# A decode step of attention and a dense layer: the result on four partitions of two column groups, two stores, and held weights for w2's last row

## The chip, the core and the metric

The kernel runs on one core of a Trainium2 chip. Such a core has a matrix engine (TensorE, in the profile PE, its weight loads PEld), a vector engine (VectorE, DVE), a scalar engine (ScalarE, ACT), GpSimd (POOL), and SyncE (SP), which here issues nearly all transfers. The engines run side by side, each through its own queue in order, and wait for each other on semaphores. SBUF is the working memory of 128 partitions; PSUM, also of 128 partitions, takes what TensorE computes. The metric is the time of one execution on the device in microseconds (us). A profiled execution has a time of its own, and a span, which is the part of it that the trace shows.

## The reference

Two batch rows, one new token each. `A` is attention over a cache of 4096 positions with 32 heads of 128, `B` a dense layer with ReLU, and a gate mixes the two.

```python
def _A_ref(x, k_cache, v_cache, wq, wo):        # x 2x1x512, caches 2x32x4096x128
    q = (x @ wq).reshape(B, Sq, Hq, Dh) -> b h q d
    scores = jnp.einsum("bhqd,bhkd->bhqk", q, k) * (Dh ** -0.5)
    p = _softmax(scores, axis=-1)
    o = jnp.einsum("bhqk,bhkd->bhqd", p, v)
    return o.transpose(0, 2, 1, 3).reshape(B, Sq, Hq * Dh) @ wo
def _B_ref(x, w1, w2):                          # w1 512x1376, w2 1376x512
    return jnp.maximum(x @ w1, 0) @ w2
g = _sigmoid((A_x * gate_w).sum(-1, keepdims=True))
return g * a + (1 - g) * b                      # 2x1x512, bf16
```

## The kernel before

Every operation is recorded by a helper in the queue of its engine, in the order in which the code is written; a named marker becomes a semaphore value that others wait for. There is no planner: the written order is the order of each queue.

SP issues the loads one after the other (L282 to L295): wq, w1, twenty-one pieces of the K and V caches, the first 96 rows of w2 (`w2x`, two transfers of twelve rows in SBUF from a three by four cut in DRAM, L289), wo in two parts (rows 0 to 23 and 24 to 31 of each partition's 32, `WO_CUT` = 24), and the rest of w2 in three parts (`w2b` rows 0 to 6, `w2c` rows 7 and 8, `w2d` row 9). Pieces share regions of one SBUF buffer, so each load waits until the piece before it in its region has been read; w2's last parts wait only for their turn. The store is SP's last transfer (L296), and SP then waits for it to be received (L298).

The computation: `gate` makes the gate and some constants on VectorE from an identity matrix that POOL fills in (L232 to L260, a list of memsets and selects; `sel2`, a two-column selector, is reduced on VectorE in L326). `q_proj` and `ffn_h` are the first products; `ffn_relu` (L406) writes the hidden row of the dense layer, already multiplied with 1 - g, into `hT` (128 partitions, 14 columns, 2 batch rows). Then 64 turns of K: VectorE transposes (L417), TensorE makes scores. Softmax, then eleven pieces of V: products on TensorE (L510), extraction on VectorE (L518, L521).

The tail, in TensorE's order, after V's last piece:

- `project(range(-4, 0))`: the four rows of `w2x` with `hT`, into one PSUM bank, each row in one column group of the array (`tile_position=(0, 32 * t)`, result on partitions 32t and 32t+1), 512 columns wide (L564).
- `o_gather`, `o_scale`, `o_turn`: the attention result, normed and gated, is turned and cast by VectorE (L552) into `oW` (128 partitions, 32 rows, 2 batch rows).
- `project(range(24))`: wo's rows 0 to 23 in the same way into the same bank (L564), which VectorE then copies to SBUF as `pr_sb` in fp32 (`pr_copy`, L569).
- `last_rows`: `fin_row` for wo's rows 24 to 31, then one for `pr_sb` with `sel2` (it adds the four column groups of the bank; fp32), then ten for w2's rows 0 to 9 with `hT`. Each `fin_row` is four matmuls of 128 columns (L573): the c-th quarter of the 512 outputs goes through column group c onto partitions 32c and 32c+1. Every matmul brings its own weight load, two columns.
- `store`: four casts of 2x128 from PSUM to `out_sb` (2x512), two after each other on VectorE (L592) and two on ScalarE (L594). Each raises the semaphore `fin`; SP stores at 4.

`mm_held` (L421) makes a matmul that uses the weights already in the array; the products with `xTw` and the K scores use it. A weight load of its own is `ldweights`.

Of the kernel before, what the change touches and what calls it, by code (L numbers as in the profile page):

```python
# [14 lines left out]
HALF = 16384  # L15
REGION = {"A": 0, "Ah": HALF, "B": 2 * HALF, "C": 4 * HALF}
WO_CUT = 24


class _Marker:  # L20
# [67 lines left out]
def bass_gated_mix__gqa_block_cached__dense_activation_relu__decode_kernel(  # L88
# [50 lines left out]
    nrow = sb("nrow", [128, 8, 4], dt.float32)  # L139
    negm = sb("negm", [128, 32], dt.float32)  # L140
    lsum = sb("lsum", [128, 2, 2], dt.float32)
    sel2 = sb("sel2", [128, 2], dt.float32)
    lrow = sb("lrow", [128, 2], dt.float32)
    rinv = sb("rinv", [32, 2], dt.float32)
    mask8 = sb("mask8", [128, 8], dt.bfloat16)
# [3 lines left out]
    sell_odd = sell[:, 1:65].rearrange("p (u f two) -> p u f two", u=8, two=2)[:, :, :, 0]  # L149
    s4 = sb("s4", [32, 4, 128], dt.bfloat16)  # L150
    O_sb = sb("O_sb", [32, 2, 128], dt.bfloat16)
    oW = sb("oW", [128, 32, 2], dt.bfloat16)
    hT = sb("hT", [128, 14, 2], dt.bfloat16)
    out_sb = sb("out_sb", [2, 512], dt.bfloat16)
    w2x = sb("w2x", [128, 4, 512], dt.bfloat16)
    hrowT = kt[:, 2, 0:448]

# [21 lines left out]

    for e in ("pe", "dve", "act", "pool"):  # L180
        P.sems[e] = nc.alloc_semaphore(e + "_ev")
    names = ["x", "gw", "wq", "w1", "wo0", "wo1", "w2x", "w2b", "w2c", "w2d", "out", "fin"]
    sem = {n: nc.alloc_semaphore("sem_" + n) for n in names}
    sem_region = {r: nc.alloc_semaphore("sem_region" + r) for r in REGION}

# [7 lines left out]
        return m  # L193


    both, lo, hi = (0, 1), (0,), (1,)
    k_pieces = [(0, both, "A"), (1, both, "B"), (2, lo, "C"), (3, both, "A"), (4, both, "B"), (2, hi, "C"),
                (5, both, "A"), (6, both, "B"), (7, lo, "C"), (7, hi, "A")]
# [30 lines left out]
    def pe(fn, waits=(), signal=None, dwaits=()):  # L229
# [4 lines left out]
    pool(lambda g: g.affine_select(out=ident16[:], in_=ident16[:], pattern=[[-1, 128]],  # L234
                                   compare_op=ALU.not_equal, fill=1.0, base=0, channel_multiplier=1),
         waits=["c_i16z"], signal="c_i16")
    pool(lambda g: g.memset(xTw[:], 0.0), signal="c_xTw")
    pool(lambda g: g.memset(qbuf[:], 0.0), signal="c_qbuf")  # L238
    pool(lambda g: g.memset(mpad[:], 0.0), signal="c_mpad")
    pool(lambda g: g.memset(w2x[:], 0.0), signal="c_w2x")  # L240
    pool(lambda g: g.memset(sell[:], 0.0), signal="c_s0")  # L241
    pool(lambda g: g.memset(sell_odd, 1.0), waits=["c_s0"], signal="c_s1")
# [50 lines left out]
    sp(lambda e: e.dma_start(wreg[:, 512 * WO_CUT:HALF], wo_in[:, 512 * WO_CUT:HALF]).then_inc(sem["wo1"], 16))  # L293
    for name, r0, r1 in (("w2b", 0, 7), ("w2c", 7, 9), ("w2d", 9, 10)):
        sp(lambda e, name=name, r0=r0, r1=r1: e.dma_start(w2[:, r0:r1, :], w2_in[:, r0:r1, :]).then_inc(sem[name], 16))  # L295
    sp(lambda e: e.dma_start(out.rearrange("b s n -> (b s) n"), out_sb[:, :]).then_inc(sem["out"], 16),  # L296
       dwaits=[(sem["fin"], 4)])
    sp(lambda e: e.wait_ge(sem["out"], 16))  # L298


    def gate():
        for t in range(4):
            pe(lambda e, t=t: e.transpose(PSB[0:128, XT_B0 + 4 * t:XT_B0 + 4 * t + 3], x_sb[0:3, t::4], ident16[0:3, 0:3]),  # L303
               waits=(["c_i16"] if t == 0 else []), dwaits=([(sem["x"], 16), (sem["gw"], 16)] if t == 0 else []),
               signal=("pe_xT" if t == 3 else None))
        dve(lambda v: v.tensor_copy(out=xT3[:, :, 0:3], in_=PSB[0:128, XT_B0:XT_B0 + 16].rearrange("p (t b) -> p t b", t=4)[:, :, 0:3]),  # L306
            waits=["pe_xT"], signal="dve_xT")
        dve(lambda v: v.tensor_copy(out=xTw[:, :, 0:2], in_=xT), waits=["dve_xT", "c_xTw"], signal="dve_xTw")
        dve(lambda v: v.tensor_tensor(out=xg[:], in0=xT, in1=xT3[:, :, 2:3].to_broadcast([128, 4, 2]), op=ALU.mult),
            waits=["dve_xT"], signal="dve_xg")  # L310
        dve(lambda v: v.tensor_reduce(out=xgs[:], in_=xg[:].rearrange("p t b -> p b t"), axis=AX.X, op=ALU.add),
            waits=["dve_xg"], signal="dve_xgs")
        pe(lambda e: e.matmul(psf(0, 128, G_C0, 2), lhsT=ones32[:, :], rhs=xgs[:, :], start=True, stop=True),
           waits=["dve_xgs", "c_ones"], signal="pe_z")
        act(lambda a: a.activation(out=ez[:], in_=psf(0, 128, G_C0, 2), func=ACT.Exp, scale=-1.0),
            waits=["pe_z"], signal="act_ez")
        dve(lambda v: v.tensor_scalar(out=ez1[:], in0=ez[:], scalar1=1.0, scalar2=None, op0=ALU.add),
            waits=["act_ez"], signal="dve_ez1")
        dve(lambda v: v.reciprocal(out=gb[:], in_=ez1[:]), waits=["dve_ez1"], signal="dve_g")
        dve(lambda v: v.tensor_scalar(out=gm[:], in0=gb[:], scalar1=-1.0, scalar2=1.0, op0=ALU.mult, op1=ALU.add),  # L320
            waits=["dve_g"], signal="dve_gm")
        dve(lambda v: v.tensor_reduce(out=maskc[:], in_=ident16[:].rearrange("p (k c) -> p c k", c=4), axis=AX.X, op=ALU.add),
            waits=["c_i16"], signal="dve_maskc")
        dve(lambda v: v.tensor_reduce(out=selx[:, 24:32], in_=ident16[:].rearrange("p (t h c) -> p h t c", t=4, c=4),
                                      axis=AX.XY, op=ALU.add), waits=["c_i16", "c_selx"], signal="dve_selx")
        dve(lambda v: v.tensor_reduce(out=sel2[:], in_=ident16[:].rearrange("p (t q) -> p q t", t=4)[:, 0:2, :], axis=AX.X, op=ALU.add),  # L326
            waits=["c_i16"], signal="dve_sel2")

    def q_window(b, blk, par, u):
        h = 2 * (blk % 2) + par  # L330
# [72 lines left out]
    def ffn_relu():  # L403
        dve(lambda v: v.transpose(out=hrowT, in_=psf(0, 128, HR_C0, 448)), waits=["pe_h"], signal="dve_hrT")
        for b in range(2):
            dve(lambda v, b=b: v.tensor_scalar(out=hT[:, :, b], in0=hrowT[:, b:448:32], scalar1=0.0,  # L406
                                               scalar2=gm[:, b:b + 1], op0=ALU.max, op1=ALU.mult),
                waits=["dve_hrT", "dve_gm"], signal=f"dve_h{b + 1}")


    def k_turn(i):
# [6 lines left out]
            waits=([f"pe_sc_{i - NKT}"] if i >= NKT else ["dve_h2"] if i == 2 else []), dwaits=([landed["k", n]] if first else []),  # L418
            signal=(f"k_read_{n}" if turn_end[n] == i else f"kt_{i}"))

    def mm_held(e, out, lhsT, rhs, start, stop, size=(128, 128), at=(0, 0)):  # L421
        a = e.lower_ap(rhs)
        w = e.lower_ap(lhsT, for_matmul_weights=True)
        return e.add_instruction(mybir.InstMatmult(  # L424
            start_tensor_calc=start, stop_tensor_calc=stop, tile_size=size, tile_position=at, ldweights=False,
            name=nc.get_next_instruction_name(), engine=mybir.EngineType.PE, ins=[a, w], outs=[e.lower_ap(out)]))

    def k_scores(i):
# [118 lines left out]
    def o_turn():  # L547
        for dq in range(4):
            pe(lambda e, dq=dq: e.matmul(psf(0, 128, R_C0, 64), lhsT=s4[:, dq, :], rhs=O_sb[:, :, 32 * dq:32 * dq + 32],
                                         start=(dq == 0), stop=(dq == 3), tile_position=(0, 0)),  # L550
               waits=(["dve_O0", "dve_O1", "c_s4"] if dq == 0 else []), signal=("pe_R" if dq == 3 else None))
        dve(lambda v: v.tensor_copy(out=oW[:, :, :].rearrange("p r b -> p b r"), in_=psf(0, 128, R_C0, 64).rearrange("p (b r) -> p b r", b=2)),  # L552
            waits=["pe_R"], signal="dve_oW")

    def pr_clear():
        dve(lambda v: v.memset(psf(0, 128, PR_C0, 512), 0.0), waits=["act_exp3"], signal="dve_pr0")
# [1 line left out]
    def project(rows):  # L558
        for r in rows:
            t = r % 4  # L560
            lhsT, rhs = (hT[:, 14 + r, :], w2x[:, t, :]) if r < 0 else (oW[:, r, :], wreg[:, r * 512:(r + 1) * 512])
            dw = {-4: [(sem["w2x"], 32)], 0: [(sem["wo0"], 16)]}.get(r, [])
            waits = {-4: ["dve_h2", "dve_pr0"], 0: ["dve_oW"]}.get(r, [])
            pe(lambda e, t=t, r=r, lhsT=lhsT, rhs=rhs: e.matmul(psf(32 * t, 32 * t + 2, PR_C0, 512), lhsT=lhsT, rhs=rhs,  # L564
                                                               start=(r < 0), stop=(r >= WO_CUT - 4), tile_position=(0, 32 * t)),
               dwaits=dw, waits=waits, signal=("pe_pr" if r == WO_CUT - 1 else None))

# [1 line left out]
        dve(lambda v: v.tensor_copy(out=pr_sb, in_=psf(0, 128, PR_C0, 512)), waits=["pe_pr"], signal="dve_pr")  # L569

    def fin_row(first, last, lhsT, rhs, dw, waits, signal):
        for c in range(4):
            pe(lambda e, c=c: e.matmul(psf(32 * c, 32 * c + 2, FIN_C0, 128), lhsT=lhsT, rhs=rhs[:, c * 128:(c + 1) * 128],  # L573
                                       start=first, stop=last, tile_position=(0, 32 * c), skip_group_check=True),
               dwaits=(dw if c == 0 else []), waits=(waits if c == 0 else []), signal=(signal if c == 3 else None))

    def last_rows():
        for r in range(WO_CUT, 32):
# [1 line left out]
        fin_row(False, False, sel2[:, :], pr_sb, [], ["dve_pr", "dve_sel2"], None)  # L580
        for r in range(10):
            dw = {0: [(sem["w2b"], 16)], 7: [(sem["w2c"], 16)], 9: [(sem["w2d"], 16)]}.get(r, [])
            fin_row(False, r == 9, hT[:, r, :], w2[:, r, :], dw, [], "pe_fin" if r == 9 else None)

    def store():
        def piece(c):
            return out_sb[:, 128 * c:128 * c + 128], psf(32 * c, 32 * c + 2, FIN_C0, 128)

        for c in range(4):
            dst, src = piece(c)  # L590
            if c < 2:
                dve(lambda v, dst=dst, src=src: v.tensor_copy(out=dst, in_=src).then_inc(sem["fin"], 1), waits=["pe_fin"])  # L592
            else:
                act(lambda a, dst=dst, src=src: a.activation(out=dst, in_=src, func=ACT.Copy).then_inc(sem["fin"], 1), waits=["pe_fin"])  # L594


    gate()
# [64 lines left out]
```

## Time and profile before

| what | us |
|---|---|
| time, median of 3 runs | 344.44 (344.37 to 344.48) |
| profiled execution: its time | 344.36 |
| profiled execution: its span in the trace | 343.0 |
| TensorE busy | 199.7 |
| VectorE busy | 192.9 |
| ScalarE busy | 15.0 |
| POOL busy | 9.5 |
| transfers: 145.43 MB read, over the span | 424 GB/s |
| mean granted clock of TensorE, share of full speed | 0.806 |

The table gives busy times of engines that work side by side, so they don't add up to the span. The 1.4 us between span and time lie before the first and after the last recorded instruction. The page lists the chain of work that ended last: followed back from the last instruction, each step goes to what released it. The share of a line in that chain, not its busy time, tells what it contributes to the time. A timeline line has the start from the span's begin, the duration, engine, line, operation, result and operands with their shapes (128x512 is partitions by elements), a count, and in brackets the idle time before it with what ended it. SPq and ACTq are the issuing of transfers by SP and ACT. The end of a matmul is modelled, its start is recorded.

### The profile page before, as it was taken

What the parts mean: (1) busy time and instruction counts of PE and PEld (TensorE: products, weight loads), DVE (VectorE), ACT (ScalarE), POOL (GpSimd) and SP (SyncE); (2) the same over time, 40 slices, a digit from 0 to 9 for tenths busy, and PEclk for the clock granted to TensorE, in tenths of its full rate; (3) what the DMA queues carried; (4) which work ended last, traced back from release to release, by engine and by line L of the source; (5) the groups of instructions that cost most, each with busy time, mean ns of one, the idle gap of its engine ahead of it and who ended that gap; (6) DMA issues with size and microseconds to landing.
All of it is one profiled execution on the core that took longest, in us unless ns stands there. A gap on an engine that the chain in (4) does not pass through costs nothing.

```text
span 343.0 us, 2484 instructions
## 1 busy us (share of the span) xinstructions
PE 199.7 (58%) x1232; PEld 52.2 (15%) x952; DVE 192.9 (56%) x136; ACT 15.0 (4%) x54; POOL 9.5 (3%) x21
## 2 busy tenths in 40 slices
PE   0440596998797996988999274005065043143656
PEld 0110121111111111111111031002023011021312
DVE  0240896996998996989999596304016103031221
ACT  1040001010001001000000300000000000000000
POOL 8200000000000000000000000000000000000000
PEclk9995599899898999999999767558568656587656
DMA  7998989999999989999999999999999999999996
GB/s 306 470 489 367 489 367 426 432 482 413 443 428 426 485 383 466 390 417 430 428 428 478 436 407 482 405 459 407 405 428 461 420 443 436 397 434 436 419 418 243
DMA packets 4081, 145.57 MB, mean 424 GB/s; under 512 B 459, under 2 KB 592, under 8 KB 872
## 3 DMA queue, kind: packets, MB, share of 16 engines
q1 hardware_dynamic: 4066, 145.43, 98.5%
q8 instruction: 8, 0.13, 0.2%
q14 instruction: 1, 0.01, 0.0%
q10 hardware_dynamic: 6, 0.00, 0.0%
HBM read 145.43 MB, written 0.00 MB: 424 GB/s over the span
## 4 chain that ended last, share of the span: by engine, by line
DMA 65%; PE 17%; DVE 15%; ACT 1%; SPq 0%; issue 0%; DVEq 0%
DMA kv<-in_A_k_cache_dram 27%; DMA kv<-in_A_v_cache_dram 26%; DVE kt L417 12%; DMA kv<-in_B_w_dram 8%; PE PS L510 5%; PE PS L424 5%; PE PS L445 5%; DMA kv<-in_A_wq_dram 4%; PE PS L344 1%; DVE kt L492 1%; ACT kt L465 1%; DVE qrow L368 1%; DVE mpad L453 1%; DVE kt L469 0%; PE PS L371 0%
## 5 line engine op out<-in xcount | busy, mean ns | idle before, releaser
L417 DVE STREAM_TRANSPOSE kt<-kv 128x2048 f32<-128x2048 f32 x64 | 141.1, 2273 | 23.0 <-DMA kv<-in_A_k_cache_dram 23.0
L445 PE MATMUL PS<-kt,qbuf 128*128 128x512 bf16 x256 | 106.1, 414 | 32.8 <-DVE kt L417 27.8
L424 PE MATMUL PS<-kt,qbuf 128*128 128x512 bf16 x256 | 105.5, 412 | 0.0
L510 PE MATMUL PS<-kv,kt 128*32 128x512 bf16 x512 | 46.1, 534 | 90.0 <-DMA kv<-in_A_v_cache_dram 77.1
L518 DVE TENSOR_TENSOR qbuf<-PS,maskc 128x512 f32<-128x512 f32 x11 | 7.6, 692 | 95.8 <-PE PS L510 95.7
L445 PEld LDWEIGHTS PS<-kt,qbuf 128*128 128x128 bf16 x256 | 25.6, 100 | 141.7 <-DVE kt L417 72.8
L510 PEld LDWEIGHTS PS<-kv,kt 128*32 128x32 bf16 x512 | 17.7, 125 | 116.8 <-issue 74.8
L492 DVE TENSOR_TENSOR kt<-kt,mask 128x512 bf16<-128x512 bf16 (+1 forms) x17 | 19.3, 1179 | 0.0
L339 ACT ACTIVATE qbuf<-PS 32x4 bf16<-32x4 bf16 (+1 forms) x40 | 7.6, 190 | 107.9 <-PE PS L424 105.9
L521 DVE TENSOR_REDUCE qbuf<-qbuf 128x128 f32<-128x512 f32 x11 | 11.3, 1025 | 0.4
L344 PE MATMUL PS<-kv,xTw 128*32 128x512 bf16 (+1 forms) x32 | 5.3, 690 | 3.3 <-DMA kv<-in_A_wq_dram 3.3
L594 ACT ACTIVATE out_sb<-PS 2x128 bf16<-2x128 f32 x2 | 0.5, 271 | 144.6 <-PE PS L573 144.6
L537 PE MATMUL PS<-qbuf,selx 128*32 128x128 f32 x22 | 4.9, 387 | 2.0 <-DVE qbuf L521 2.0
L368 DVE CAST qrow<-PS 128x256 bf16<-128x256 f32 x2 | 2.6, 1516 | 5.5 <-PE PS L424 5.5
L465 ACT ACTIVATE kt<-PS,negm 128x512 bf16<-128x512 f32 x4 | 2.7, 686 | 58.9 <-DVE negm L461 58.9
L303 PE MATMUL PS<-ident,x_sb 3*128 3x3 bf16 x4 | 0.3, 166 | 8.1 <-POOL sell L241 8.1
L306 DVE COPY xT<-PS 128x12 bf16<-128x12 bf16 x1 | 0.2, 170 | 8.4 <-PE PS L303 8.4
L238 POOL MEMSET qbuf<- 128x5120 bf16 x1 | 4.4, 4361 | 0.0
L537 PEld LDWEIGHTS PS<-qbuf,selx 128*32 128x32 f32 x22 | 3.4, 162 | 4.6 <-DVE qbuf L521 3.2
L424 PE MATMUL PS<-kv,xTw 128*32 128x512 bf16 (+1 forms) x24 | 3.7, 511 | 0.0
L453 DVE TENSOR_REDUCE mpad<-PS 128x2 f32<-128x2048 f32 x1 | 2.3, 2291 | 2.2 <-PE PS L424 2.2
L469 DVE STREAM_TRANSPOSE kt<-kt 128x1024 bf16<-128x1024 bf16 x2 | 2.5, 1246 | 1.6 <-ACT kt L465 1.5
(67 smaller groups left out, 32.3 us busy)
## 6 DMA issues: line engine op xcount, KB each, us to landing
kv<-in_A_v_cache_dram SPq DMA_DIRECT2D x6, 4096.0 KB, 36.9
kv<-in_A_k_cache_dram SPq DMA_DIRECT2D x4, 4096.0 KB, 31.7
kv<-in_A_wq_dram SPq DMA_DIRECT2D x1, 4096.0 KB, 12.2
kv<-in_A_wo_dram SPq DMA_DIRECT2D x1, 3072.0 KB, 23.4
kv<-in_B_w_dram SPq DMA_DIRECT2D x1, 1376.0 KB, 15.1
kv<-in_A_wo_dram SPq DMA_DIRECT2D x1, 1024.0 KB, 25.5
kv<-in_B_w_dram SPq DMA_DIRECT2D x1, 896.0 KB, 27.2
kv<-in_B_w_dram SPq DMA_DIRECT2D x1, 256.0 KB, 27.4
```

What stands on the lines that cost most here:

```text
L339: act(lambda a: a.activation(out=out, in_=src, func=ACT.Copy), waits=waits, signal=f"q_{b}_{u}_{blk}_{par}")
L344: return e.matmul(out, lhsT=xTw[:, t, :], rhs=rhs, start=(t == 0), stop=(t == 3), tile_position=(0, 32 * c))
L368: dve(lambda v, dst=dst, src=src: v.tensor_copy(out=dst, in_=src), waits=[f"pe_qr{half}"], signal=f"qrow{half}{e2}")
L417: dve(lambda v: v.transpose(out=dst, in_=pairs[:, h, 64 * a:64 * a + 64, :]), waits=([f"pe_sc_{i - NKT}"] if i >= NKT else ["dve_h2"] if i ...
L424: return e.add_instruction(mybir.InstMatmult(start_tensor_calc=start, stop_tensor_calc=stop, tile_size=size, tile_position=at, ldweights=F ...
L445: return e.matmul(out, lhsT=lhsT, rhs=rhs, start=start, stop=stop)
L465: act(lambda a, g=g, par=par: a.activation(out=E_sb[:, 32 * g:32 * g + 32, 16 * par:16 * par + 16], in_=psf(0, 128, (2 * par + g) * BANK, ...
L492: dve(lambda v: v.tensor_tensor(out=out, in0=src.unsqueeze(2).to_broadcast(shape), in1=mask8[:].unsqueeze(1).unsqueeze(3).to_broadcast(sha ...
L510: pe(lambda e, j=j, t=t: e.matmul(psf(32 * t, 32 * t + 32, V_BS[n % 2] * BANK, 512), lhsT=v_weights(n)[:, j], rhs=rows[:, :, j, :], start= ...
L518: dve(lambda e: e.tensor_tensor(out=parts, in0=psf(0, 128, V_BS[n % 2] * BANK, 512).rearrange("p (c d) -> p c d", c=4), in1=maskc[:].unsqu ...
L521: dve(lambda e: e.tensor_reduce(out=X2[:, b, k, :], in_=parts.rearrange("p c d -> p d c"), axis=AX.X, op=ALU.add), waits=[f"dve_m{n}"], si ...
L537: pe(lambda e, n=n, w0=w0: e.matmul(psf(0, 32, O_C0, 128), lhsT=selx[:, w0:w0 + 32], rhs=X2[:, b, n - mine[0], :], start=(n == mine[0]), s ...
```

## The change

The 512 outputs of a batch row are now cut into two halves, one per column group (g = 0 and 1), and each half into two quarters (k = 0 and 1). Both quarters of a half stand on the same 128 PSUM columns, on neighbouring partitions: batch row b and quarter k on partition 32g + 2b + k. To reach them, the weights have zeros between the two batch columns: `oW`, `hT` and `sel2` are five columns wide with the batch rows in columns 1 and 3 (`BOTH`), and a window of four columns that begins at column 1 - k puts the rows on the partitions of quarter k, zeros on those of the other. So a `fin_row` is still four matmuls, two after each other in each of two column groups, and the second of them adds to what the first wrote. POOL clears the three tensors (three memsets more, ahead of existing ones; `hT` is 18 rows long now).

w2's last row (`held_row`) differs: the weights for k = 0 are loaded by two `ldweights` of 32 columns that wait for nothing, and the two matmuls of k = 0, which wait for `w2d`, use them; the two of k = 1 bring their own loads, behind.

The store has one cast of 4x128 on VectorE, after which SP stores four rows, and one of 4x128 on ScalarE, after which ScalarE itself stores four rows. In DRAM each store writes two by two rows of 128 elements (256 B), where the old one wrote two rows of 512 (1024 B). SP waits for both at the end.

```diff
+NB = 2
+NG = 4 // NB
+WIDE = 3 * NB - 1
...
-    sel2 = sb("sel2", [128, 2], dt.float32)
+    sel2 = sb("sel2", [128, WIDE], dt.float32)
...
-    oW = sb("oW", [128, 32, 2], dt.bfloat16)
-    hT = sb("hT", [128, 14, 2], dt.bfloat16)
-    out_sb = sb("out_sb", [2, 512], dt.bfloat16)
+    oW = sb("oW", [128, 32, WIDE], dt.bfloat16)
+    hT = sb("hT", [128, 18, WIDE], dt.bfloat16)
+    out_sb = sb("out_sb", [32 * NG, 128], dt.bfloat16)
...
+    BOTH = slice(NB - 1, 2 * NB, NB)
...
+    pool(lambda g: g.memset(sel2[:], 0.0), signal="c_sel2")
     pool(lambda g: g.memset(xTw[:], 0.0), signal="c_xTw")
     pool(lambda g: g.memset(qbuf[:], 0.0), signal="c_qbuf")
     pool(lambda g: g.memset(mpad[:], 0.0), signal="c_mpad")
+    pool(lambda g: g.memset(hT[:], 0.0), signal="c_hT")
+    pool(lambda g: g.memset(oW[:], 0.0), signal="c_oW")
...
-    sp(lambda e: e.dma_start(out.rearrange("b s n -> (b s) n"), out_sb[:, :]).then_inc(sem["out"], 16),
-       dwaits=[(sem["fin"], 4)])
+    out_rows = out.rearrange("b s (g k n) -> g (b s) k n", g=2, k=2)
+    sp(lambda e: e.dma_start(out_rows[0], out_sb[0:4, :]).then_inc(sem["out"], 16), dwaits=[(sem["fin"], 1)])
     sp(lambda e: e.wait_ge(sem["out"], 16))
+    sp(lambda e: e.wait_ge(sem["out2"], 16))
...
     def fin_row(first, last, lhsT, rhs, dw, waits, signal):
-        for c in range(4):
-            pe(lambda e, c=c: e.matmul(psf(32 * c, 32 * c + 2, FIN_C0, 128), lhsT=lhsT, rhs=rhs[:, c * 128:(c + 1) * 128],
-                                       start=first, stop=last, tile_position=(0, 32 * c), skip_group_check=True),
-               dwaits=(dw if c == 0 else []), waits=(waits if c == 0 else []), signal=(signal if c == 3 else None))
+        for n in range(4):
+            k, g = divmod(n, NG)
+            pe(lambda e, k=k, g=g: e.matmul(psf(32 * g, 32 * g + 2 * NB, FIN_C0, 128), lhsT=lhsT[:, NB - 1 - k:3 * NB - 1 - k],
+                                            rhs=rhs[:, (NB * g + k) * 128:(NB * g + k + 1) * 128], start=(first and k == 0),
+                                            stop=(last and k == NB - 1), tile_position=(0, 32 * g), skip_group_check=True),
+               dwaits=(dw if n == 0 else []), waits=(waits if n == 0 else []), signal=(signal if n == 3 else None))
+
+    def held_row(dw):
+        for g in range(NG):
+            pe(lambda e, g=g: e.ldweights(hT_cols(9 * WIDE + NB - 1), tile_position=(0, 32 * g)))
+        for n in range(4):
+            k, g = divmod(n, NG)
+
+            def fn(e, k=k, g=g):
+                out, rhs = psf(32 * g, 32 * g + 2 * NB, FIN_C0, 128), w2[:, 9, (NB * g + k) * 128:(NB * g + k + 1) * 128]
+                lhsT = hT[:, 9, NB - 1 - k:3 * NB - 1 - k]
+                if k == 0:
+                    return mm_held(e, psf(32 * g, 32 * g + 32, FIN_C0, 128), hT_cols(9 * WIDE + NB - 1), rhs, False, False, (128, 32), (0, 32 * g), True)
+                return e.matmul(out, lhsT=lhsT, rhs=rhs, start=False, stop=(k == NB - 1), tile_position=(0, 32 * g), skip_group_check=True)
+            pe(fn, dwaits=(dw if n == 0 else []), signal=("pe_fin" if n == 3 else None))
+
+    def hT_cols(c0):
+        return hT[:, :, :].rearrange("p r c -> p (r c)")[:, c0:c0 + 32]
...
-            fin_row(False, r == 9, hT[:, r, :], w2[:, r, :], dw, [], "pe_fin" if r == 9 else None)
+            if r == 9:
+                held_row(dw)
+            else:
+                fin_row(False, False, hT[:, r, :], w2[:, r, :], dw, [], None)
 
     def store():
-        def piece(c):
-            return out_sb[:, 128 * c:128 * c + 128], psf(32 * c, 32 * c + 2, FIN_C0, 128)
-
-        for c in range(4):
-            dst, src = piece(c)
-            if c < 2:
-                dve(lambda v, dst=dst, src=src: v.tensor_copy(out=dst, in_=src).then_inc(sem["fin"], 1), waits=["pe_fin"])
-            else:
-                act(lambda a, dst=dst, src=src: a.activation(out=dst, in_=src, func=ACT.Copy).then_inc(sem["fin"], 1), waits=["pe_fin"])
+        dve(lambda v: v.tensor_copy(out=out_sb[0:4, :], in_=psf(0, 4, FIN_C0, 128)).then_inc(sem["fin"], 1), waits=["pe_fin"])
+        act(lambda a: a.activation(out=out_sb[32:36, :], in_=psf(32, 36, FIN_C0, 128), func=ACT.Copy), waits=["pe_fin"], signal="act_out")
+        act(lambda a: a.dma_start(out_rows[1], out_sb[32:36, :]).then_inc(sem["out2"], 16), waits=["act_out"])
```

Left out of the diff: the writers of `sel2`, `hT` and `oW` (L326, L406, L552) now write to `BOTH` and wait for the memsets, `project` reads its weights with `BOTH`, and `mm_held` has a parameter more.

More of the change, by code (lines that the diff above doesn't have):

```diff
@@ L181, in bass_gated_mix__gqa_block_cached__dense_activation_relu__decode_kernel @@
         P.sems[e] = nc.alloc_semaphore(e + "_ev")
-    names = ["x", "gw", "wq", "w1", "wo0", "wo1", "w2x", "w2b", "w2c", "w2d", "out", "fin"]
+    names = ["x", "gw", "wq", "w1", "wo0", "wo1", "w2x", "w2b", "w2c", "w2d", "out", "out2", "fin"]
     sem = {n: nc.alloc_semaphore("sem_" + n) for n in names}
@@ L325, in gate @@
                                       axis=AX.XY, op=ALU.add), waits=["c_i16", "c_selx"], signal="dve_selx")
-        dve(lambda v: v.tensor_reduce(out=sel2[:], in_=ident16[:].rearrange("p (t q) -> p q t", t=4)[:, 0:2, :], axis=AX.X, op=ALU.add),
-            waits=["c_i16"], signal="dve_sel2")
+        dve(lambda v: v.tensor_reduce(out=sel2[:, BOTH], in_=ident16[:].rearrange("p (t q) -> p q t", t=4)[:, 0:2, :], axis=AX.X, op=ALU.add),
+            waits=["c_i16", "c_sel2"], signal="dve_sel2")
     def q_window(b, blk, par, u):
@@ L405, in ffn_relu @@
         for b in range(2):
-            dve(lambda v, b=b: v.tensor_scalar(out=hT[:, :, b], in0=hrowT[:, b:448:32], scalar1=0.0,
+            dve(lambda v, b=b: v.tensor_scalar(out=hT[:, 0:14, NB - 1 + NB * b], in0=hrowT[:, b:448:32], scalar1=0.0,
                                                scalar2=gm[:, b:b + 1], op0=ALU.max, op1=ALU.mult),
-                waits=["dve_hrT", "dve_gm"], signal=f"dve_h{b + 1}")
+                waits=["dve_hrT", "dve_gm", "c_hT"], signal=f"dve_h{b + 1}")
     def k_turn(i):
@@ L419, in k_turn, with mm_held @@
             signal=(f"k_read_{n}" if turn_end[n] == i else f"kt_{i}"))
-    def mm_held(e, out, lhsT, rhs, start, stop, size=(128, 128), at=(0, 0)):
+    def mm_held(e, out, lhsT, rhs, start, stop, size=(128, 128), at=(0, 0), skip=False):
         a = e.lower_ap(rhs)
@@ L424, in mm_held @@
         return e.add_instruction(mybir.InstMatmult(
-            start_tensor_calc=start, stop_tensor_calc=stop, tile_size=size, tile_position=at, ldweights=False,
+            start_tensor_calc=start, stop_tensor_calc=stop, tile_size=size, tile_position=at, ldweights=False, bass_skip_group_check=skip,
             name=nc.get_next_instruction_name(), engine=mybir.EngineType.PE, ins=[a, w], outs=[e.lower_ap(out)]))
@@ L551, in o_turn @@
                waits=(["dve_O0", "dve_O1", "c_s4"] if dq == 0 else []), signal=("pe_R" if dq == 3 else None))
-        dve(lambda v: v.tensor_copy(out=oW[:, :, :].rearrange("p r b -> p b r"), in_=psf(0, 128, R_C0, 64).rearrange("p (b r) -> p b r", b=2)),
-            waits=["pe_R"], signal="dve_oW")
+        dve(lambda v: v.tensor_copy(out=oW[:, :, BOTH].rearrange("p r b -> p b r"), in_=psf(0, 128, R_C0, 64).rearrange("p (b r) -> p b r", b=2)),
+            waits=["pe_R", "c_oW"], signal="dve_oW")
     def pr_clear():
@@ L560, in project @@
             t = r % 4
-            lhsT, rhs = (hT[:, 14 + r, :], w2x[:, t, :]) if r < 0 else (oW[:, r, :], wreg[:, r * 512:(r + 1) * 512])
+            lhsT, rhs = (hT[:, 14 + r, BOTH], w2x[:, t, :]) if r < 0 else (oW[:, r, BOTH], wreg[:, r * 512:(r + 1) * 512])
             dw = {-4: [(sem["w2x"], 32)], 0: [(sem["wo0"], 16)]}.get(r, [])
```

## The prediction

> **What bounds the kernel now.** I read the granted clock first (mean 0.806 of full speed), then the page's chain (DMA 65% of the span), then the end of that chain in order of time, columns start, duration, what:
>
> ```profile
> 313.39 27.43 DMA kv<-in_B_w_dram
> 340.82 0.04 issue
> 340.86 0.26 PE PS L573 x4
> 341.12 0.02 issue
> 341.14 0.28 DVE out_sb L592
> 341.42 0.03 issue
> 341.45 0.28 DVE out_sb L592
> ```
>
> Until 340.82 us the loads set the time; the last one is w2's last row (w2d). Only what follows it can be shortened: four matmuls, two casts one after the other on VectorE (two on ScalarE beside them), the store. The timeline of the tail shows what stands before and after:
>
> ```profile
> 337.63 1.07 PE L573 MATMUL PS<-kv,oW 128*2 128x128 bf16 x32
> ...
> 338.64 0.61 PE L573 MATMUL PS<-qbuf,sel 128*2 128x128 f32 x8
> ...
> 339.70 0.56 PE L573 MATMUL PS<-kv,hT 128*2 128x128 bf16 x28 [0.44 <-DMA kv<-in_B_w_dram]
> ...
> 340.86 0.09 PEld L573 LDWEIGHTS PS<-kv,hT 128*2 128x2 bf16 x4 [0.40 <-DMA kv<-in_B_w_dram]
> 340.86 0.23 PE L573 MATMUL PS<-kv,hT 128*2 128x128 bf16 x4 [0.22 <-DMA kv<-in_B_w_dram]
> ...
> 341.76 0.28 SPq L296 DMA_DIRECT2D out_dram<-out_sb  x1
> ```
>
> The reader is to see that TensorE waits for data in this tail, and that 32 matmuls of 311 ns take only 1.07 us: the four column groups stream side by side. The third view is the clock (PEclk), by stretches:
>
> ```profile
> core 0: us, PE busy (x) PEld busy (x) DVE busy (x) ACT busy (x) POOL busy (x), PEclk, DMA share, GB/s
> 308.88:312.29 3.41, 2.68 (x28) 0.86 (x20) 0.69 (x1) 0.00 (x0) 0.00 (x0) 0.50 0.96 413
> ...
> 329.36:332.78 3.42, 2.39 (x24) 0.61 (x16) 1.37 (x2) 0.00 (x0) 0.00 (x0) 0.50 1.02 438
> ...
> 336.19:339.60 3.41, 3.06 (x56) 1.26 (x48) 0.69 (x1) 0.00 (x0) 0.00 (x0) 0.50 0.90 359
> 339.60:343.00 3.40, 1.07 (x40) 0.57 (x40) 0.56 (x2) 0.54 (x2) 0.00 (x0) 1.00 0.09 27
> ```
>
> TensorE ran at half clock until 339.60 and at full clock after. Last, the issues of transfers on SP and ACT, and SP's wait for the store:
>
> ```profile
> 0.79 0.55 ACTq L280 DMA_DIRECT2D x_sb<-in_A_x_dram  x1
> ...
> 1.37 0.23 ACTq L281 DMA_DIRECT2D x_sb<-in_gate_w_dram  x1
> ...
> 286.59 0.87 SPq L289 DMA_DIRECT2D w2x<-in_B_w_dram  x1
> ...
> 287.51 0.72 SPq L289 DMA_DIRECT2D w2x<-in_B_w_dram  x1
> ...
> SPq L298 <- DMA out_dram<-out_sb: 0.9, 1, 0.9
> ```
>
> The two L289 issues cost SP 0.87 and 0.72 us, the other loads 0.33 to 0.43. In the code they are the only ones whose two sides are cut differently: twelve rows in SBUF against three by four in DRAM. The old store (two rows on both sides) cost 0.28.
>
> **The change, part by part.** The sum is made against the profiled execution: 344.36 us, of which 342.97 are the span (343.0 on the page). The median of the runs is 344.44, 0.08 above.
>
> Second casts: the store waited for the second cast, 341.45 against 341.14. One cast of four partitions has the same 128 elements per partition and is taken at the same 0.28. **-0.31**.
>
> Half the column groups. A row of fin_row now has two matmuls after each other in each of two column groups, where four stood side by side. At half clock one step of 128 columns costs (1.07 - 0.311)/7 = 0.108, at full clock (0.56 - 0.219)/6 = 0.057 (the 0.219 is the duration of one of those matmuls); by the starts of the matmuls it is 0.107 and 0.055, which I use. The fp32 row (two passes per matmul) takes (0.61 - 0.20)/2 = 0.21 per pass at half clock, 0.20 being what a bf16 matmul of 0.311 has over its step. From 337.63 on: 8 wo rows x 2 x 0.107 = 1.71, to 339.34; four fp32 passes, 0.26 of that work at half clock until 339.60, the remaining 0.58 in 0.29, to 339.89; nine w2 rows x 2 x 0.055 with some 2 ns each, 1.01, to 340.90. w2d is there at 340.86. So a reserve is eaten up: before, TensorE had done rows 0 to 8 by 340.64. **+0.04**. Then w2d's own second step, at full clock: **+0.055**. If the step from fp32 to bf16, which now follows without a pause, drained the array, or the cast into oW (L552, 0.23) grew with its step of five elements, the slot is later: at the 5.9 ns per element of the strided cast L368 (1.52 us for 256), 64 elements take 0.38, so 0 to +0.15; I take 0, nearer to L552 itself, which writes with a step already.
>
> Weights already loaded. From w2d's release (340.86) to the cast (341.14) are 0.28. The matmul alone is 0.22, and from the last project matmul (337.20 + 0.64) to its reader at 337.90 are 0.06, with weights loaded long before. So the load costs at most about 0.01 today. Bounds 0 to -0.08 (its recorded duration); I take **0**.
>
> The stores. Each has four rows in SBUF against two by two in DRAM, the form of L289. Bounds: 0.28 (the old store) and 0.87, the first of its kind on its queue, as ACT's store is; with ACT's first issue against its second (0.55, 0.23) on top, 1.2. I take 0.87 for ACT: 0.87 - 0.28 = **+0.59**. SP's store (0.72 to 0.87) runs beside it. ACT's wait for its own cast is taken like SP's for VectorE's (0.03); POOL's wait for itself at 1.14 was 0.23, so up to +0.2. Behind ACT's DMA nothing is queued; behind SP's the waits for both stores, the second **+0.04** (one "issue" step). Receipt stays 0.9.
>
> The Trainium skill (DMA: Bandwidth & Descriptors, Specifications) says that transfers below 512 B make the DMA engine read, modify and write. Output rows fall from 1024 to 256 B. No run shown here has a store that small; by the page's HBM latency (0.2 us on average, section Latency and other measured facts) the estimate would be 0.2 more.
>
> Start of the program. Three memsets on POOL (sel2, hT, oW; 128x128 takes 0.20, 128x32 0.12) push all later POOL work by some 0.5. The last, selx, ends at 10.8 to 11.3; VectorE's reductions L324 and L326 follow, and VectorE's next work is L368 at 16.74, behind wq's landing at 13.03. That covers it; uncovered it would be 0.5. hT is written at 24 us, before a VectorE that idles for K. SP's load queue is not moved past.
>
> Sum: -0.31 + 0.04 + 0.055 + 0.59 + 0.04 = +0.4, from 344.36 to **344.8**, slightly slower, but within 0.2% (0.69 us, about what a measurement of this kernel can tell from no change).
>
> **The rivals.** B, the store costs no more to issue than the old one (0.28 to 0.45): the sum without the 0.59 is -0.18, 344.2. For it: only four short rows, two of L289's needs (twelve rows, the other load ahead) are gone. Against: loads of 128 rows with one cut cost 0.33, so the number of rows is not what made 0.87.
>
> C, slower: TensorE becomes the bound. In this execution the full clock begins at 339.60, in time by 0.04. The clock rose after stretches with 2.68 and 3.06 of 3.41 us busy, not after 2.39. If the grid of these stretches can lie elsewhere, the rise falls between about 337.4 (2.68 busy since 335.12, with 0.39 before it) and 340.8. With the rise at e the slot of w2d is at (342.1 + e)/2, 342.1 being the sum at half clock (1.71 + 0.84 + 18 x 0.107 from 337.63). It decides from e = 339.6 on: e = 340.7 gives 341.4, 0.5 late, 345.3. If two streaming groups count only half as busy, the clock may not rise at all: w2d at 342.1 (+1.2), its second step and last matmul at half clock (+0.14): 346.1. Before, a late rise cost little, since TensorE was 0.22 ahead. The Trainium skill (TensorE: Matmul & The Clock Gate, Part 1) has the window free-running, 3.4 us, and run-variable; the 3.41 us stretches agree, and by it 1.2 of 3.41 of the executions come late.
>
> E, the 256 B rows cost another trip to memory: up to the 0.9 of the receipt, 345.7. Nothing in the trace speaks for or against it; the rule cited above does for it.
>
> **How the numbers follow.** A 0.50, C 0.28 (0.35 of grid positions are late, some too little to tell), B 0.14, E 0.08. The time is A's, 344.8, own range 344.5 to 345.1. The range reaches down to B (344.1 leaves out little of it) and up through C and E to 345.9; without rise the time is above it. Slower by over 0.2% (above 345.13): C 0.22, E 0.07, A with ACT's issue at 1.2 and a late slot 0.06: 0.35. Faster by over 0.2% would need 0.69 where all savings make 0.31 and at most 0.08: 0.03 for what I don't see. Within: 0.62.
>
> **What would show it.** In the profile after: one cast of about 0.28 each; the stores' issues at 0.7 to 0.9 against 0.28; fin_row's 32 wo matmuls over 1.8 us instead of 1.07; w2's last matmuls starting within 0.1 of w2d's landing if the clock rises by 339.7, later by half of any delay. The prediction is wrong if the stores issue in 0.3 us, if rows 0 to 8 are done well before w2d, or if the wait for the stores grows from 0.9.

## The result, and the profile after

The changed kernel takes 345.13 us (median of 19 runs, 344.84 to 345.99) where the kernel before takes 344.36 beside it (19 runs, 344.26 to 344.60). The ratio is 1.0024, 95% interval 1.0017 to 1.0030: 0.6 to 1.0 us slower. The profiled execution took 345.07, its span is 343.6.

The end of the chain of waits of the changed kernel, as shown for the kernel before (start, duration, what):

```profile
312.57 25.10 DMA kv<-in_A_wo_dram
337.67 0.04 issue
337.72 3.36 PE PS L582 x76
341.08 0.06 PE PS L432 x2
341.13 0.07 PE PS L598 x2
341.21 0.02 issue
341.23 0.28 DVE out_sb L616
```

The reader is to see two things. Only one cast is left in it (0.28 where there were two). And w2d's landing, which ended the loads before, is not in it: from the landing of wo's second part on, the chain runs on TensorE, 76 matmuls of `fin_row` and the held row behind them. The timeline of the tail of the same execution:

```profile
337.72 1.77 PE L582 MATMUL PS<-kv,oW 128*4 128x128 bf16 x32
...
339.32 0.60 PE L582 MATMUL PS<-qbuf,sel 128*4 128x128 f32 x8
339.91 0.98 PEld L582 LDWEIGHTS PS<-kv,hT 128*4 128x4 bf16 x36 [0.28 <-DMA kv<-in_B_w_dram]
339.91 1.17 PE L582 MATMUL PS<-kv,hT 128*4 128x128 bf16 x36
...
340.91 0.22 PE L432 MATMUL PS<-kv,hT 128*32 128x128 bf16 x2
...
340.97 0.22 PE L598 MATMUL PS<-kv,hT 128*4 128x128 bf16 x2
341.23 0.27 ACT L617 ACTIVATE out_sb<-PS 4x128 bf16<-4x128 f32 x1 [144.36 <-PE PS L598]
341.23 0.28 DVE L616 CAST out_sb<-PS 4x128 bf16<-4x128 f32 x1 [2.91 <-PE PS L598]
341.53 0.72 ACTq L618 DMA_DIRECT2D out_dram<-out_sb  x1
341.54 0.68 SPq L304 DMA_DIRECT2D out_dram<-out_sb  x1
```

The 32 wo matmuls take 1.77 instead of 1.07. The weight loads of w2's rows waited 0.28 for w2b (it landed at 339.87 in the trace), and the rows start right behind it, at 339.91. The chain passes over this wait, because the modelled end of the fp32 row (339.93) lies as late. The casts begin at 341.23 (before: 341.14) and end at 341.51 (before: 341.73), so up to here the change has gained 0.22. The stores' issues last 0.72 and 0.68 where the one store took 0.28. SP's waits, a third view, have the rest (total, times, longest):

```profile
SPq L306 <- DMA out_dram<-out_sb: 1.4, 1, 1.4
```

It was 0.9. From the end of the casts to the end of the span there are 2.13 now, 1.23 before: the store gave back the 0.22 and 0.68 more, which is the growth of the span; the remaining 0.03 of the 0.71 between the two profiled executions lie outside it.

### The profile page after: what moved, and what is told of

Read it like the earlier page. It is cut to its first block, busy times and chain, and to the rows that moved or that the text cites. A ratio compares the mean times of both kernels' runs of the same rounds, so it can differ in the third digit from the quotient of the medians.

```text
span 343.6 us, 2486 instructions
## 1 busy us (share of the span) xinstructions
PE 200.3 (58%) x1232; PEld 53.5 (16%) x952; DVE 192.8 (56%) x135; ACT 14.7 (4%) x53; POOL 9.8 (3%) x24
## 4 chain that ended last, share of the span: by engine, by line
DMA 74%; PE 15%; DVE 10%; issue 0%; SPq 0%; DVEq 0%
DMA kv<-in_A_v_cache_dram 35%; DMA kv<-in_A_k_cache_dram 27%; DVE kt L425 9%; DMA kv<-in_A_wo_dram 7%; PE PS L432 5%; PE PS L453 4%; DMA kv<-in_A_wq_dram 4%; PE PS L518 3%; PE PS L352 1%; PE PS L582 1%; DVE qrow L376 1%; PE PS L379 0%; SPq L298 0%; DVE out_sb L616 0%; PE PS L598 0%
## 5 line engine op out<-in xcount | busy, mean ns | idle before, releaser
L518 PE MATMUL PS<-kv,kt 128*32 128x512 bf16 x512 | 47.3, 546 | 89.3 <-DMA kv<-in_A_v_cache_dram 80.5
L545 PE MATMUL PS<-qbuf,selx 128*32 128x128 f32 x22 | 3.9, 325 | 2.2 <-DVE qbuf L529 2.2
```

The costliest lines, as they stand in the source:

```text
L518: pe(lambda e, j=j, t=t: e.matmul(psf(32 * t, 32 * t + 32, V_BS[n % 2] * BANK, 512), lhsT=v_weights(n)[:, j], rhs=rows[:, :, j, :], start= ...
L545: pe(lambda e, n=n, w0=w0: e.matmul(psf(0, 32, O_C0, 128), lhsT=selx[:, w0:w0 + 32], rhs=X2[:, b, n - mine[0], :], start=(n == mine[0]), s ...
```

## The experiments

**same_cut**: the changed kernel, its stores cut evenly.

```diff
-rhs=rhs[:, (NB * g + k) * 128:(NB * g + k + 1) * 128]
+rhs=rhs[:, (NG * k + g) * 128:(NG * k + g + 1) * 128]
...
-    out_rows = out.rearrange("b s (g k n) -> g (b s) k n", g=2, k=2)
+    out_rows = out.rearrange("b s (k g n) -> g (b s k) n", g=2, k=2)
```

> Changed kernel, but the quarters are dealt out alternately (output columns 256k + 128g), so that each of the two stores has four evenly spaced rows on both sides; 256 B rows, two queues and TensorE's work stay. Theory 1, the uneven cut is what made the issues 0.68 and 0.72 us: both issues fall to about 0.28, their packets start about 0.5 after the issue instead of 0.64 and 0.97, time 344.2 to 344.6. Rival 2, a second store in flight (ScalarE's queue) or the 256 B rows cost the time: the issues may get short, but ScalarE's packets still come 0.3 later than SP's, time 344.7 to 345.0.

Measured: 344.43 (344.27 to 345.25), ratio 1.0001 (0.9993 to 1.0010), 0.7 below the changed kernel. Its timeline, and SP's wait:

```profile
341.10 0.27 ACT L617 ACTIVATE out_sb<-PS 4x128 bf16<-4x128 f32 x1 [144.28 <-PE PS L598]
341.10 0.28 DVE L616 CAST out_sb<-PS 4x128 bf16<-4x128 f32 x1 [2.43 <-PE PS L598]
341.39 0.27 ACTq L618 DMA_DIRECT2D out_dram<-out_sb  x1
341.40 0.30 SPq L304 DMA_DIRECT2D out_dram<-out_sb  x1
```

```profile
SPq L306 <- DMA out_dram<-out_sb: 1.0, 1, 1.0
```

Still two queues and rows of 256 B, but the issues are back at 0.27 and 0.30, the wait at 1.0. From the end of the casts to the end of the span there are 1.38, against 2.13 in the changed kernel and 1.23 before. So 0.75 of the 0.90 that the stores cost is the cut; at most 0.15 is left for the number of stores and the length of their rows. ScalarE's first packet comes 0.11 before SP's here (342.15 and 342.25, the times of the packets in the trace); in the changed kernel it comes 0.36 after (343.22 and 342.86).

**one_store** and **one_store_odd**: TensorE's part of the change and one cast per engine, but a single store of four rows of 512 B; evenly cut in the one, and in the other with the partitions in the order quarter, batch row, so that its DRAM side needs two by two. In both the quarters are dealt out as in same_cut.

```diff
+        dve(... out=out_sb[:, 0:128], in_=psf(0, 4, FIN_C0, 128)).then_inc(sem["fin"], 1), waits=["pe_fin"])
+        act(... out=out_sb[:, 128:256], in_=psf(32, 36, FIN_C0, 128), func=ACT.Copy).then_inc(sem["fin"], 1), waits=["pe_fin"])
...
-    sp(lambda e: e.dma_start(out_rows[0], out_sb[0:4, :]).then_inc(sem["out"], 16), dwaits=[(sem["fin"], 1)])
+    sp(lambda e: e.dma_start(out.rearrange("b s (k n) -> (b s k) n", k=2), out_sb[:, :]).then_inc(sem["out"], 16), dwaits=[(sem["fin"], 2)])
```

```diff
-BOTH = slice(NB - 1, 2 * NB, NB)
+BOTH = slice(2, 4)
...
-lhsT=lhsT[:, NB - 1 - k:3 * NB - 1 - k]
+lhsT=lhsT[:, 2 - 2 * k:6 - 2 * k]
...
-out.rearrange("b s (k n) -> (b s k) n", k=2)
+out.rearrange("b s (k n) -> k (b s) n", k=2)
```

> TensorE's part of the change and its one cast per engine, but both casts go to the same four partitions side by side and SP alone stores four evenly spaced rows of 512 B. Theory 1: the gain of the second cast (-0.31) comes out, less 0.1 for TensorE's second step and its later slot: 344.1 to 344.3, below the kernel before. Rival 3, TensorE's half column groups are the main cost: 344.6 or more, and w2's last row starts late in the trace.

> As one_store, the same four rows of 512 B, but partitions in the order quarter, batch row (weights with two zero columns on either side), so that the four rows in SBUF stand against two by two in DRAM. Only the cut differs. Theory 1: issue 0.7 instead of 0.28 and a later first packet, 0.4 to 0.6 above one_store. Rival 2 (second queue, 256 B rows): equal to one_store within 0.1.

Measured: one_store 344.53 (344.01 to 345.38), ratio 1.0005 (0.9996 to 1.0013); one_store_odd 344.85 (344.46 to 345.78), ratio 1.0013 (1.0004 to 1.0022). The store's issue and SP's wait of one_store, then of one_store_odd:

```profile
341.47 0.30 SPq L303 DMA_DIRECT2D out_dram<-out_sb  x1
...
SPq L304 <- DMA out_dram<-out_sb: 0.9, 1, 0.9
```

```profile
341.61 0.68 SPq L303 DMA_DIRECT2D out_dram<-out_sb  x1
...
SPq L304 <- DMA out_dram<-out_sb: 1.1, 1, 1.1
```

The same bytes in the same rows: the uneven cut alone adds 0.38 to the issue and 0.16 behind it (the first packet comes 0.64 after the issue's end instead of 0.48), 0.54 in the trace. The medians are only 0.3 apart, below the forecast 0.4 to 0.6, for both kernels scatter over more than 1.3 us. one_store's forecast of 344.1 to 344.3 missed: its fastest execution is at 344.01, its median above the kernel before. Two things lie between. Some executions are slow because of the clock, which is rival 3 in part, as the next runs show. And in eight of its twelve executions 1.7 to 1.9 us lie outside the span, where the kernel before has 1.3 to 1.6 (last section). Its median span is 342.85, that of the kernel before beside it 343.0.

**act_store_only**: the changed kernel without SP's store.

> The changed kernel without SP's store: only the second half of each output row is written, by ScalarE. In the changed kernel ScalarE's packets start 0.97 us after its issue, SP's 0.64 after theirs. If two uneven stores at once are prepared one after the other, ScalarE's packets start 0.64 after the issue here and the end is 0.3 earlier; if ScalarE's queue is slower by itself, 0.97 stays.

Measured (one execution): 344.77. The timeline of its store:

```profile
341.48 0.73 ACTq L616 DMA_DIRECT2D out_dram<-out_sb  x1
```

The first packet comes 0.65 after the issue's end, where it was 0.97 with SP's store beside it. ScalarE's queue is no slower by itself: SP's uneven store beside it holds it up by 0.3. From the begin of the cast to the end of the span are 2.08, in the changed kernel 2.41.

**before_two_stores**: the kernel before, with only its store divided between SP and ScalarE, evenly cut.

```diff
+    sp(lambda e: e.dma_start(out_rows[:, 0:256], out_sb[:, 0:256]).then_inc(sem["out"], 16), dwaits=[(sem["fin"], 2)])
...
+        act(lambda a: a.dma_start(out_rows[:, 256:512], out_sb[:, 256:512]).then_inc(sem["out2"], 16), waits=["act_out2", "act_out3"])
```

> The kernel before, with only its store divided: SP stores the left half of both rows after VectorE's two casts, ScalarE the right half after its own two; two rows of 512 B each, evenly cut on both sides. Theory 1: no cost beyond 0.05, 344.3 to 344.45. Rival 2, the second store in flight lands later: its packets come 0.3 after SP's, 344.6 to 344.8.

Measured: 344.49 (344.38 to 344.72), ratio 1.0001 (0.9992 to 1.0009), just above the forecast and below the rival's. ScalarE's first packet comes 0.11 before SP's (342.42 and 342.52), not 0.3 after. From the end of the casts to the end of the span are 1.32 instead of 1.23. In the time, a second even store costs nothing that can be told here.

**changed_warm** and **one_store_warm**: twelve matmuls without use, to raise the clock ahead of the tail.

```diff
+    def warm():
+        for j in range(12):
+            t = j % 4
+            pe(lambda e, t=t: e.matmul(psf(32 * t, 32 * t + 32, 2 * BANK, 512), lhsT=ident16[:, 0:32], rhs=w2x[:, t, :], start=True, stop=True,
+                                       tile_position=(0, 32 * t)))
...
     project(range(-4, 0))
+    warm()
```

> The changed kernel with twelve matmuls more (512 columns, weights from the identity, into an unused PSUM bank), put behind w2x's four, where TensorE otherwise waits for VectorE from about 331.8 to 333. Their results are not used. They only keep TensorE busy, so that its clock is full before the tail. Theory C (the clock, which rises late in some executions, sets when w2's last row is done): the upper executions of the changed kernel (345.4 to 346.0) vanish, spread below 0.4, median 344.8 to 345.0. Rival, the spread is of the transfers or the stores: spread and median stay (345.1, up to 346).

> one_store (344.53, 344.01 to 345.38) with the same twelve matmuls. Theory C: spread below 0.4 and median 344.1 to 344.25, below the kernel before. Rival: as one_store, and TensorE's two column groups cost a fixed amount.

Measured: changed_warm 345.01 (344.75 to 345.41), ratio 1.0015 (1.0007 to 1.0024); one_store_warm 344.41 (343.95 to 344.70), ratio 0.9996 (0.9987 to 1.0005). The upper executions are nearly gone: of the changed kernel five of 19 lay above 345.40 (345.41, 345.45, 345.50, 345.65, 345.99), of one_store three of twelve above 345.00; with the matmuls there is one (345.41) and none. The two other pairs with and without these matmuls agree: same_cut has two of eleven above 344.8 and one_store_28, below, five of eleven at 345.0 or more; with the matmuls their highest are 344.51 and 344.87. The runs of the changed kernel say the same from the other side: its five slowest have mean granted clocks of 0.791 to 0.802 and spans of 343.9 to 344.6, the fourteen others 0.806 to 0.841 and 343.4 to 343.7. So the late clock is shown as the cause of the upper tail. Both medians fall by 0.12, which is within the intervals.

The forecasts of theory C missed all the same in part: the spreads are 0.66 and 0.75, not below 0.4, and one_store_warm's median is above the forecast 344.1 to 344.25. Its spans are 342.6 to 342.9 in all eleven executions, so what scatters there lies outside the span. Nor do the matmuls keep the clock full through the tail everywhere: in changed_warm's profile it is at half from 335.34 to 338.75.

The profile of one_store_warm has full clock from 333.16 to the end, and shows what TensorE's tail is then:

```profile
337.67 1.06 PE L586 MATMUL PS<-kv,oW 128*4 128x128 bf16 x32 [0.93 <-DMA kv<-in_A_wo_dram]
338.50 0.36 PEld L586 LDWEIGHTS PS<-qbuf,sel 128*4 128x4 f32 x8
338.56 0.60 PE L586 MATMUL PS<-qbuf,sel 128*4 128x128 f32 x8
339.84 0.98 PEld L586 LDWEIGHTS PS<-kv,hT 128*4 128x4 bf16 x36 [0.97 <-DMA kv<-in_B_w_dram]
...
340.84 0.22 PE L430 MATMUL PS<-kv,hT 128*32 128x128 bf16 x2
```

Now the weight loads wait 0.97 for w2b, and still w2's last row starts 1.0 behind it: 18 steps of 0.055 for rows 0 to 8. In this execution w2d lands 0.98 after w2b (339.80, 340.78), and so it does in the other profiles, 0.97 to 0.99, those of before_warm and before_two_stores among them. Only the profile of the kernel before, from which the prediction was made, has 1.17 (339.65, 340.82). Two column groups use up the usual distance whatever the clock was before.

**one_store_28**: one_store with wo's rows 24 to 27 in `project`; **one_store_28_warm**: the same with the twelve matmuls.

```diff
+FIN_R0 = 28
...
-        for r in range(WO_CUT, 32):
+        for r in range(FIN_R0, 32):
...
-    project(range(WO_CUT))
+    project(range(FIN_R0))
```

> one_store with wo's rows 24 to 27 taken by project (four column groups, 512 columns) instead of fin_row, behind the same load: 0.43 instead of 0.85 us of TensorE at half clock, 0.3 less until w2d. Theory C: executions with a late clock lose some 0.3 less, median 344.3, highest below 345.1. Rival: as one_store.

> one_store_28 with the twelve unused matmuls. If what is left of one_store_warm's spread (343.95 to 344.70) comes from executions in which TensorE is still behind w2d, it shrinks to the lower half, median 344.1 to 344.2; if it lies outside TensorE, it stays at 344.4.

Measured: one_store_28 344.54 (344.07 to 345.31), ratio 1.0007 (0.9998 to 1.0016), a miss: the work saved before the fp32 row is spent in waiting for VectorE's copy (0.24 of idle ahead of it in the trace). Its profiled execution is one with a late clock, by stretches:

```profile
336.60:340.05 3.45, 3.45 (x45) 1.69 (x38) 0.69 (x1) 0.00 (x0) 0.00 (x0) 0.50 0.85 334
340.05:342.90 2.85, 1.29 (x42) 1.11 (x38) 0.28 (x1) 0.27 (x1) 0.00 (x0) 1.00 0.02 6
```

With the rise at 340.05, w2's last row starts at 341.06, 0.27 after w2d's landing in this execution (340.79): theory C in one picture. one_store_28_warm took 344.38 (344.12 to 344.87), ratio 0.9998 (0.9989 to 1.0007), the time that was given for scatter outside TensorE. Its spans lie between 342.7 and 343.0.

**warm_not_held**: one_store_warm with w2's last row like the others (`fin_row` for r = 9 too).

> one_store_warm (344.41, 343.95 to 344.70) with w2's last row as the other rows: no weights loaded ahead. Prediction's reading, the load costs at most 0.01: the same time within 0.1, and from w2d's release to the casts 0.28 plus 0.055 for the second step. Rival, the load's recorded 0.08 stands in the way of the first matmul: 0.08 later from release to cast, 344.5.

Measured: 344.57 (343.99 to 344.74), ratio 1.0000 (0.9991 to 1.0009). Both variants of this pair fall into two clumps, near 344.1 and 344.55, and the medians differ by how many fell into which; the spans have the same median, 342.7. In the traces the first matmul of w2's last row starts 0.32 before the casts in both. TensorE comes to this row without a pause in both, so the pair shows no gain of the held weights here; what they are worth where TensorE has to wait for w2d, the case that they were made for, no run shows.

**before_warm**: the kernel before with the twelve matmuls.

> The kernel before with the twelve unused matmuls of one_store_warm. Theory C as predicted, TensorE was 0.2 ahead of w2d there, so the clock decides nothing but the last four matmuls (0.31 instead of 0.22): 344.3 to 344.5, as before. Rival, the twelve matmuls help by themselves (for example through a faster chain to wo): 0.1 or more below the kernel before.

Measured: 344.40 (344.23 to 344.73), ratio 1.0000 (0.9991 to 1.0009). They bring nothing to the kernel before.

**same_cut_warm**: both costs taken away from the changed kernel.

> same_cut (344.43, 344.27 to 345.25) with the twelve unused matmuls: the changed kernel with both of its costs taken away, the uneven cut and the late clock. If these two are the whole loss, the time is 344.2 to 344.35 with no execution above 344.8, that is the kernel before less what the second cast gave (0.31), plus TensorE's second step and the second store (0.15 together). If something else in the change costs, it stays at 344.4 or above the kernel before.

Measured: 344.33 (344.19 to 344.51; 11 runs), ratio 0.9998 (0.9989 to 1.0007). It is 0.8 below the changed kernel, none of its executions is above 344.51, and nothing of the loss is left that could be told, though the interval leaves room for 0.3. No version is measurably faster than the kernel before; the lowest ratio is one_store_warm's, and its interval holds 1. In the span, though, one_store_warm is 0.3 shorter (median 342.7 over eleven executions, 343.0 over the 27 of the kernel before beside it), which is what the second cast was forecast to give. The time outside the span takes it back.

## Why the prediction was right in its direction, and too small

The sign and the place were as forecast, and the time lies in the range; but the likeliest case ended within 0.2%, the kernel is 0.24% slower, and 345.13 lies just above that case's own range of 344.5 to 345.1. Of the signs that the prediction named for its being wrong, one came: the wait for the stores grew from 0.9, to 1.4. By the steps:

- **Second casts, -0.31**: as forecast. The end of the casts is 0.22 earlier and their begin 0.09 later, which makes the 0.31.
- **Half the column groups, +0.04 and +0.055**: measured together 0.09, but by another way, so that the fit is partly luck. The profiled execution had its clock up at 339.25, earlier than the one before (339.60), and w2's last row was late all the same, since w2b landed at 339.87 and 18 steps follow. I had these rows wait only for TensorE's own work (339.89 in the sum, with w2b there at 339.70), and I took the landing of w2d from that one execution, where it comes 1.17 after w2b's; it is 0.98 here. The cast into oW grew to 0.34, near its bound of 0.38. It is hidden, for TensorE's wait behind it is ended by the landing of wo's first part (335.19):

```profile
334.60 0.34 DVE L560 CAST oW<-PS 128x64 bf16<-128x64 f32 x1 [0.38 <-PE PS L557]
...
335.32 2.27 PE L572 MATMUL PS<-kv,oW 128*2 128x512 bf16 x24 [0.76 <-DMA kv<-in_A_wo_dram]
```

- **Weights already loaded, 0**: agrees with warm_not_held; with a wait for w2d in front it was not tested.
- **The stores' issue, +0.59**: the rows that it was read from (L289) were the right ones, the size too high: 0.40 on SP, 0.44 on ScalarE. ScalarE's first uneven issue has no surcharge.
- **"Receipt stays 0.9"**: this is the step that failed. The end of the span comes 1.39 after the end of ScalarE's issue, 0.92 after the end of the old store's. one_store_odd puts 0.16 of it on the uneven cut itself, act_store_only 0.3 on two such stores at once. The term "store" was 0.63 with the second wait; it is 0.9.
- **Rival C**: it is a part of the result, not another result. Five of 19 executions above 345.40 against the forecast share of 0.35 that come late. That two streaming groups count only half for the clock is refuted, though not by the changed kernel: before its rise at 339.25, TensorE is busy 3.28 of 3.41, of which 1.53 (from 337.72 on) with two groups. Counted half, that would be 2.5, which lies between the 2.39 and the 2.68 of the prediction's stretches and decides nothing. The profile of one_store_28_warm decides. Before its rise at 339.66 it has 2.96, of which 1.49 (from 338.17 on) with two groups; counted half, 2.2, less than the 2.39 after which the clock did not rise. The two stretches, in the columns of the prediction's third view, the changed kernel first:

```profile
335.84:339.25 3.41, 3.28 (x50) 1.84 (x43) 0.69 (x1) 0.00 (x0) 0.00 (x0) 0.50 0.95 381
...
336.25:339.66 3.41, 2.96 (x38) 1.35 (x32) 0.69 (x1) 0.00 (x0) 0.00 (x0) 0.50 0.88 357
```

- **Rival B** (the store no dearer) fell with the issues of 0.72 and 0.68. **Rival E**, the 256 B rows, fell with same_cut, which has them. The Trainium skill (DMA: Bandwidth & Descriptors, Specifications) has transfers below 512 B read, modify and write. No run here shows a price for it: with rows of 256 B the wait for both stores is 1.0 (same_cut), with rows of 512 B as well (before_two_stores).
- **Start of the program**: no sign of the three memsets in the chain, as forecast.

What stays open: that one uneven store holds up the other is shown, by one execution, but not in which unit; nor is it known why an uneven cut costs more.

## What to carry to other kernels

Cut both sides of a transfer alike: four evenly spaced rows against two by two rows cost 0.54 us here, 0.75 with two at once, and the issue's duration in the timeline tells it at a glance. A change that moves work onto fewer column groups is paid where the reserve ahead of the last load was, so measure the distance between landings, not TensorE's idle share. Where a reserve depends on when the clock rises or on the distance between two landings, look at many executions: one profile shows one case of each. And compare the spans beside the times: here a gain of 0.3 in the span did not arrive in the time.

## What was not expected of the hardware

Two even stores from SP and ScalarE send their first packets 0.11 apart, two uneven ones 0.36. The kernels with a single store of four 512 B rows fall into two clumps (one_store_warm: 343.95 to 344.11 and 344.30 to 344.70, 0.45 apart). The profiles of one_store (344.48) and one_store_warm (344.04) have spans of 342.7 each, so this lies outside the span, 1.8 against 1.35. All executions of the six kernels of this kind agree: time less span is 1.3 to 1.45 in 29 of them and 1.7 to 2.0 in 37, while no execution of the kernel before, of the changed kernel or of another one with two stores has more than 1.65. Why is open.
